# The first product of each expert from seven block products in place of eight, and the experts in two halves of d_ff

## The chip, the cores and the metric

The kernel runs on one core of a Trainium2 chip. The metric is the time of one execution on the device in microseconds (us), the median of several runs. The engines are called as in the profile: PE multiplies matrices, PEld is its loading of the stationary operand, DVE is the vector engine, ACT the scalar engine, POOL the third elementwise engine, and SP issues the DMAs.

## The reference, cut to what matters

Linear attention over 2 batches, 8 heads, 576 tokens of 64 features gives `x`, 1152 x 512. A gated layer without a nonlinearity follows, and then four experts over all tokens:

```python
x = attn_out.transpose(0, 2, 1, 3).reshape(1152, 512)
a = x @ w1; b = x @ w2                 # d_ff 1024
x = (a * b @ w3) @ w_out               # back to 512
p = domain_probs / (domain_probs.sum(-1, keepdims=True) + 1e-09)
for e in range(4):
    h = np.maximum(x @ moe2_w1[e], 0.0)        # first product:  1152 x 512 by 512 x 1024
    out += p[:, e:e + 1] * (h @ moe2_w2[e])    # second product: 1152 x 1024 by 1024 x 512
```

All inputs are float32.

## The kernel before, in words

**Numbers.** A product of float32 values is made from three matmuls. `split` turns a tile into a high part (ACT rounds it into the matmul's format, L70) and a low part (DVE subtracts that from the source, L71), and `PASSES` adds low x high, high x low and high x high in one PSUM bank. Every tile that enters a matmul has both parts, `[:, HI]` and `[:, LO]`.

**Stages.** First comes the attention, pair of heads by pair of heads, with the folding of `w3 @ w_out` beside it (`fold`, L175). Then `gated` (L148) makes `a * b` for each batch and block of d_ff, and `expert_input(b)` (L193) multiplies it by the folded weights, which gives `x2[b, j]`: for batch `b` the 128 rows `j` of d_model, transposed, 576 tokens wide. Each batch is worked in two columns of 288 tokens (`c`). From there on only the experts run.

**An expert.** For each block of 128 columns of d_ff (`g`, in two quarters `qd`), 4 banks take the first product for 2 batches x 2 columns, each from 4 blocks of d_model x 3 passes, 288 columns a matmul (L485). The two columns `c` follow each other with the same stationary tile. ACT takes relu of a bank as the high part of `hid` (L492), DVE the low part from the same bank (L493). When the 8 blocks of `hid` are there, the second product runs over 9 tiles of 128 tokens, each a chain of 24 matmuls of 512 columns (L504), and DVE adds the bank, times the expert's weight, to `acc` (L510 for the first expert, L512 for the others). After the last expert each tile of `acc` goes out by DMA (L517).

**Weights.** `load_w` brings 128 x 512 of weights by a DMA on SP into one of 4 buffers of the pool `raw` (L469) and splits it into a tile of `w1` (8 buffers, one expert's halves in turn) or `w2e` (8 buffers). The buffer of `raw` is free for the next load when the low part has been made.

**Order.** The program's text is not the order on the engines: a scheduler puts all instructions of an engine into one fixed list before the kernel runs, and each engine goes through its list without overtaking. Banks of PSUM are taken in turn: eight of them, called t, f, kv, et, f, x, w, po (f twice).

Of the kernel before, what the change touches and what calls it, by code (L numbers as in the profile page):

```python
# [8 lines left out]
F32 = mybir.dt.float32  # L9
# [26 lines left out]
def attention_moe_kernel(ctx: ExitStack, tc: tile.TileContext, q, k, v, omega, mw1, mw2, mw3, mwo, probs, ew1, ew2, out):  # L36
# [28 lines left out]
    def bank(tag):  # L65
        return ps_p.tile([P, 512], F32, tag=tag, name="ps_" + tag, bufs=BANKS[tag])
# [370 lines left out]
    a_p = mctx.enter_context(tc.tile_pool(name="a", bufs=1, reuse_waits="tile"))  # L437
# [29 lines left out]
    def load_w(pool, src, name):  # L467
        r = raw_p.tile([P, 512], F32, tag="raw", name=name + "r")
        nc.sync.dma_start(out=r, in_=src)  # L469
        t = pool.tile([P, 2, 512], F32R, tag=pool.name, name=name)  # L470
        split(t[:, HI], t[:, LO], r)
        return t

    for e in range(NE):
        hd = []
        for qd in range(EFF // 512):
            w1t = [load_w(w1_p, ew1[e, kk * P:(kk + 1) * P, qd * 512:(qd + 1) * 512], "w1") for kk in range(KD)]
            for g in range(4):
                ht = hid_p.tile([P, 2, NT], F32R, tag="hid", name="hid")
                banks = [next_bank() for _ in range(2 * B)]  # L480
                for b in range(B):
                    for kk in range(KD):
                        for n, (x, y) in enumerate(PASSES):
                            for c in range(2):
                                nc.tensor.matmul(  # L485
                                    out=banks[2 * b + c][:, :HS], lhsT=w1t[kk][:, x, g * P:(g + 1) * P],
                                    rhs=x2[b, kk][:, y, c * HS:(c + 1) * HS],
                                    start=(kk == 0 and n == 0), stop=(kk == KD - 1 and n == 2),
                                )
                for c in range(2 * B):  # L490
                    s = slice(c * HS, (c + 1) * HS)
                    nc.scalar.activation(out=ht[:, HI, s], in_=banks[c][:, :HS], func=ACTF.Relu)  # L492
# [4 lines left out]
                hd.append(ht)
        w2t = [load_w(w2_p, ew2[e, f * P:(f + 1) * P, :], "w2") for f in range(KE)]
        for t in range(NTILE):
            ps = next_bank()  # L500
            n = 0
            for f in range(KE):
                for x, y in PASSES:
                    nc.tensor.matmul(  # L504
                        out=ps, lhsT=hd[f][:, x, t * P:(t + 1) * P], rhs=w2t[f][:, y], start=(n == 0), stop=(n == 3 * KE - 1),
                    )
                    n += 1
            p_e = pr[:, t, e:e + 1]
            if e == 0:
                nc.vector.tensor_scalar(out=acc[:, t], in0=ps, scalar1=p_e, scalar2=None, op0=ALU.mult)  # L510
            else:
                nc.vector.scalar_tensor_tensor(  # L512
                    out=acc[:, t], in0=ps, scalar=p_e, in1=acc[:, t], op0=ALU.mult, op1=ALU.add,
                )
            if e == NE - 1:
                for rows, toks in out_rows(t):
                    nc.sync.dma_start(out=out[toks], in_=acc[rows, t])  # L517
# [30 lines left out]
```

## Time and profile before

| | us |
|---|---|
| median of 3 runs | 731.67 |
| lowest and highest of them | 729.31, 731.77 |
| the profiled execution | 733.19 |
| its span, first to last instruction | 731.4 |
| PE busy | 706.1 |
| DVE busy | 321.8 |
| ACT busy | 228.7 |

The profiled execution is 1.5 us above the median and 1.8 us longer than its own span. Matmuls are pipelined, and the profile shows each until its end, so that a matmul of 288 columns has a length of 295 ns while the next one starts 130 ns after it.

### The profile page before, as it was taken

How to read it: one execution, taken by the hardware profiler on the slowest of the kernel's cores; microseconds unless marked ns; L12 is line 12 of the kernel's file. 1: busy time of each engine (PE TensorE's matmuls, PEld its weight loads, DVE VectorE, ACT ScalarE, POOL GpSimd, SP SyncE). 2: the span in 40 equal slices, each digit the busy share in tenths (PEclk: the TensorE clock that was granted, in tenths of full speed). 3: DMA queues.
4: the chain of work that ended last, by engine and by line, in shares of the span. 5: the costliest groups of instructions: out<-in, count | busy, mean ns of one | idle time of the engine just before them, and what ended most of it. 6: DMA issues, size and time to landing. Idle time of an engine off the chain costs nothing.

```text
span 731.4 us, 10840 instructions
## 1 busy us (share of the span) xinstructions
PE 706.1 (97%) x4457; PEld 649.0 (89%) x4457; DVE 321.8 (44%) x620; ACT 228.7 (31%) x524; POOL 47.8 (7%) x47
## 2 busy tenths in 40 slices
PE   6879999989899999999999999999999999999997
PEld 5768888879899999999998899988899988999886
DVE  3799667689942275315331154231334311522111
ACT  4675545466422254214330033210223200322000
POOL 1130000035300041000000000000000000000000
PEclk9989999999999999999999999999999999999999
DMA  7676343345410031203110031020211200100011
GB/s 198 193 201 186 103 117 101 101 144 173 145 59 1 1 116 47 70 1 116 59 58 1 1 116 58 1 57 1 71 46 58 58 0 1 58 1 1 30 49 53
DMA packets 44129, 52.13 MB, mean 71 GB/s; under 512 B 15280, under 2 KB 31664, under 8 KB 44080
## 3 DMA queue, kind: packets, MB, share of 16 engines
q1 hardware_dynamic: 44080, 51.44, 23.4%
q8 instruction: 35, 0.57, 0.3%
q14 instruction: 14, 0.11, 0.1%
HBM read 49.07 MB, written 2.36 MB: 70 GB/s over the span
## 4 chain that ended last, share of the span: by engine, by line
PE 74%; issue 8%; DVE 8%; DMA 5%; ACT 1%; POOL 1%; DVEq 0%; POOLq 0%; SPq 0%; ACTq 0%
PE ps_f L504 7%; PE ps_f L485 7%; PE ps_po L175 5%; DMA f<-in_moe_w_dram 4%; PE ps_kv L504 4%; PE ps_et L504 4%; PE ps_po L485 3%; PE ps_x L485 3%; PE ps_et L485 3%; PE ps_t L485 3%; PE ps_w L485 3%; PE ps_kv L485 3%; PE ps_t L504 3%; PE ps_po L504 3%; PE ps_w L504 3%
## 5 line engine op out<-in xcount | busy, mean ns | idle before, releaser
L485 PE MATMUL ps_f<-x,w 128*128 128x288 f32 x384 | 102.7, 295 | 0.0
L485 PEld LDWEIGHTS ps_f<-x,w 128*128 128x128 f32 x384 | 72.3, 188 | 0.1
L70 ACT ACTIVATE w<-w2r 128x512 fp32r<-128x512 f32 x32 | 19.9, 632 | 140.1 <-PE ps_et L504 44.5
L504 PE MATMUL ps_f<-w,hid 128*128 128x512 f32 x240 | 56.1, 389 | 0.0
L504 PEld LDWEIGHTS ps_f<-w,hid 128*128 128x128 f32 x240 | 44.9, 188 | 9.2
L148 PE MATMUL ps_po<-xt,w 128*128 128x288 f32 x240 | 49.6, 305 | 2.7 <-DVE w3o L71 2.1
L485 PE MATMUL ps_w<-x,w 128*128 128x288 f32 x192 | 51.4, 295 | 0.0
L485 PE MATMUL ps_t<-x,w 128*128 128x288 f32 x192 | 51.4, 295 | 0.0
L485 PE MATMUL ps_kv<-x,w 128*128 128x288 f32 x192 | 51.4, 295 | 0.0
L485 PE MATMUL ps_po<-x,w 128*128 128x288 f32 x192 | 51.4, 295 | 0.0
L485 PE MATMUL ps_x<-x,w 128*128 128x288 f32 x192 | 51.4, 295 | 0.0
L485 PE MATMUL ps_et<-x,w 128*128 128x288 f32 x192 | 51.3, 295 | 0.0
L148 PE MATMUL ps_w<-xt,w 128*128 128x288 f32 x240 | 48.7, 297 | 0.9 <-DVE a L159 0.9
L175 PE MATMUL ps_po<-wo,w3T 128*128 128x512 f32 x192 | 48.6, 402 | 0.3 <-DVE w3T L71 0.2
L71 POOL TENSOR_TENSOR w<-w12f,w 128x512 fp32r<-128x512 f32 x24 | 35.1, 1469 | 183.7 <-ACT w L70 91.7
L175 PEld LDWEIGHTS ps_po<-wo,w3T 128*128 128x128 f32 x192 | 35.2, 188 | 8.6 <-DVE w3T L71 1.6
L148 PEld LDWEIGHTS ps_po<-xt,w 128*128 128x128 f32 x240 | 39.2, 194 | 3.4 <-DVE w3o L71 2.2
L85 DVE SCALAR_TENSOR_TENSOR f64e<-f,f64e 128x512 uint32<-128x512 uint32 x48 | 40.1, 837 | 0.6
L148 PEld LDWEIGHTS ps_w<-xt,w 128*128 128x128 f32 x240 | 38.7, 191 | 1.5 <-DVE a L159 0.7
L84 DVE TENSOR_SCALAR f64e<-f 128x512 uint32<-128x512 uint32 x48 | 24.6, 514 | 27.3 <-DMA f<-in_moe_w_dram 26.4
L485 PEld LDWEIGHTS ps_kv<-x,w 128*128 128x128 f32 x192 | 36.2, 189 | 0.0
L485 PEld LDWEIGHTS ps_w<-x,w 128*128 128x128 f32 x192 | 36.2, 189 | 0.0
(185 smaller groups left out, 1390.1 us busy)
## 6 DMA issues: line engine op xcount, KB each, us to landing
f<-in_moe_w_dram SPq DMA_DIRECT2D x40, 512.0 KB, 3.7
w1r<-in_moe_w_dram SPq DMA_DIRECT2D x32, 256.0 KB, 3.0
w2r<-in_moe_w_dram SPq DMA_DIRECT2D x32, 256.0 KB, 2.8
f<-in_moe_w_out_dram SPq DMA_DIRECT2D x8, 512.0 KB, 4.8
kr<-in_k_dram SPq DMA_DIRECT2D x8, 256.0 KB, 3.3
va<-in_v_dram SPq DMA_DIRECT2D x16, 128.0 KB, 4.0
qr<-in_q_dram SPq DMA_DIRECT2D x8, 256.0 KB, 3.7
out_dram<-acc SPq DMA_DIRECT2D x8, 256.0 KB, 2.1
```

The source lines that it names most:

```text
L70: nc.scalar.activation(out=hi, in_=src, func=ACTF.Copy)
L71: (eng or nc.vector).tensor_tensor(out=lo, in0=src, in1=hi.bitcast(F32), op=ALU.subtract)
L84: nc.vector.tensor_scalar(out=e, in0=high, scalar1=0x80000000, scalar2=None, op0=ALU.bitwise_and)
L85: nc.vector.scalar_tensor_tensor(out=e, in0=low, scalar=29, in1=e, op0=ALU.logical_shift_right, op1=ALU.bitwise_or)
L148: nc.tensor.matmul(out=bs[c][:, :HS], lhsT=w12[w, g][:, x, kk], rhs=xt[b][kk][:, y, c * HS:(c + 1) * HS], start=(kk == 0 and n == 0), stop ...
L175: nc.tensor.matmul(out=po, lhsT=wt[:, a, g * P:(g + 1) * P], rhs=wo[hf * 4 + g][:, c], start=(n == 0), stop=(n == 3 * KF - 1),)
L485: nc.tensor.matmul(out=banks[2 * b + c][:, :HS], lhsT=w1t[kk][:, x, g * P:(g + 1) * P], rhs=x2[b, kk][:, y, c * HS:(c + 1) * HS], start=(k ...
L504: nc.tensor.matmul(out=ps, lhsT=hd[f][:, x, t * P:(t + 1) * P], rhs=w2t[f][:, y], start=(n == 0), stop=(n == 3 * KE - 1),)
```

## The change: what it does

The first product of an expert is a matrix of 1024 (d_ff) x 1152 (tokens). The change cuts d_ff, d_model and the tokens in two each (the tokens by batch), so that the product is 2 x 2 blocks by 2 x 2 blocks, `A11` to `A22` of the weights (rows: half of d_ff, columns: half of d_model) and `B11` to `B22` of the tokens (rows: half of d_model, columns: batch). Written out, that is eight block products; Winograd's form has seven, with sums of the operands before and of the products behind:

- of the weights: S1 = A21 + A22, S2 = S1 - A11, S3 = A11 - A21, S4 = A12 - S2
- of the tokens: T1 = B12 - B11, T3 = B22 - B12, T2 = B22 - T1, T4 = B21 - T2
- products: P1 = A11 B11, P2 = S2 T2, P3 = S3 T3, P4 = S1 T1, P5 = A12 B21, P6 = A22 T4, P7 = S4 B22
- results: C11 = P1 + P5; u2 = P1 + P2, u3 = u2 + P3; c22 = u3 + P4, c21 = u3 + P6, c12 = u2 + P4 + P7

The sums of the tokens are made once, in `expert_input`, and those of the weights for each expert. `hidden(g, c)` makes one block of 128 rows of both halves of d_ff for one column `c` of both batches: seven products of 6 matmuls each. P5, P6 and P7 are accumulated in the banks of P1, P3 and P4, which hold their first product until ACT (for P1) or DVE (for P3 and P4) has read it. Each expert runs in two halves (`hf`): a half makes 4 of the 8 blocks of `hid` and then adds its part of the second product to `acc`, so that a chain of the second product has 12 matmuls and `acc` takes 9 additions a half.

`hid` has 4 buffers in place of 8, `w2e` 6, and the pools of the last stage lie on the other side of the memory. The core of the diff:

```diff
     def expert_input(b):
-        for j in range(KD):
-            x2[b, j] = xt_p.tile([P, 2, S], F32R, tag="xt", name="x2")
...
+                j = i // 2 + i % 2 * (KD // 2)
...
-                split(x2[b, j][:, HI, s], x2[b, j][:, LO, s], ps[:, :HS])
+                p = ps[:, :HS]
+                if b == 0:
...
+                    nc.scalar.activation(out=xf[j][:, s], in_=p, func=ACTF.Copy)
+                    put_x2(("B11", "B21")[i % 2], i // 2, s, xf[j][:, s])
+                elif i % 2 == 0:
...
+                    nc.vector.tensor_tensor(out=t1, in0=p, in1=xf[j][:, s], op=ALU.subtract)
+                    put_x2("T1", i // 2, s, t1)
+                else:
+                    b22 = temp("b22")
+                    nc.scalar.activation(out=b22, in_=p, func=ACTF.Copy)
+                    nc.vector.tensor_tensor(out=t3, in0=b22, in1=top, op=ALU.subtract)
+                    nc.vector.tensor_tensor(out=t1, in0=b22, in1=t1, op=ALU.subtract)
+                    put_x2("B22", i // 2, s, b22)
+                    put_x2("T3", i // 2, s, t3)
+                    put_x2("T2", i // 2, s, t1)
+                    nc.vector.tensor_tensor(out=t1, in0=xf[j][:, s], in1=t1, op=ALU.subtract)
+                    put_x2("T4", i // 2, s, t1)
...
+    GH = KE // 4
+    w2_p = ctx.enter_context(tc.tile_pool(name="w2e", bufs=6, side="right", reuse_waits="tile"))
+    hid_p = ctx.enter_context(tc.tile_pool(name="hid", bufs=2 * GH, side="right", reuse_waits="tile"))
...
+    def load_w1(hf):
+        raw = {}
+        for m, k in ((1, 0), (1, 1), (0, 0), (0, 1)):
+            r = raw_p.tile([P, 2, GH * P], F32, tag="raw", name="w1r")
+            f0 = m * (EFF // 2) + hf * GH * P
+            nc.sync.dma_start(
+                out=r, in_=ew1[e, k * (DM // 2):(k + 1) * (DM // 2), f0:f0 + GH * P].rearrange("(k p) f -> p k f", p=P),
+            )
+            raw[f"A{m + 1}{k + 1}"] = r
...
+            nc.vector.tensor_tensor(out=r, in0=x, in1=y, op=op)
+            w1s(name, r)
+        for name in ("A11", "A12", "A22"):
+            w1s(name, raw[name])
...
+    def hidden(g, c):
...
+        def product(ps, a, b, first=True, final=True):
+            for kk in range(2):
+                for n, (x, y) in enumerate(PASSES):
+                    nc.tensor.matmul(
+                        out=ps, lhsT=w1t[a][:, x, kk, g * P:(g + 1) * P], rhs=x2[b, kk][:, y, s],
...
+        pa, pb, pc, pd = (next_bank()[:, :HS] for _ in range(4))
+        product(pa, "A11", "B11", final=False)
+        p1 = s_p.tile([P, HS], F32, tag="p1", name="p1", bufs=2)
+        nc.scalar.activation(out=p1, in_=pa, func=ACTF.Copy)
+        product(pb, "S2", "T2")
+        u2 = total(pb, p1, "u2")
+        product(pc, "S3", "T3", final=False)
+        u3 = total(pc, u2, "u3")
+        product(pd, "S1", "T1", final=False)
+        c22 = total(pd, u3, "c22")
+        product(pa, "A12", "B21", first=False)
+        put(0, 0, pa)
+        put(1, 1, c22)
+        product(pc, "A22", "T4", first=False)
+        put(1, 0, total(pc, u2, "c21"))
+        product(pd, "S4", "B22", first=False)
+        put(0, 1, total(pd, u2, "c12"))
...
     for e in range(NE):
-        hd = []
-        for qd in range(EFF // 512):
...
+        for hf in range(2):
+            w1t, w2t = {}, []
+            load_w1(hf)
+            hd = [hid_p.tile([P, 2, NT], F32R, tag="hid", name="hid") for _ in range(2 * GH)]
+            for c in range(2):
+                for g in range(GH):
+                    hidden(g, c)
+            blocks = [m * (KE // 2) + hf * GH + g for m in range(2) for g in range(GH)]
+            w2t = [load_w2(f) for f in blocks]
...
+            for t in (0, 1, 5, 6, 2, 3, 4, 7, 8):
```

`put` is relu as the high part (ACT) and the low part (DVE) from its source, and `total` is one addition on DVE. Three places in the engines' lists show what the scheduler makes of it.

The first is PE's list at the start of the first product: of the second expert before the change, of the second half of the first expert with it. Names are bank, tokens, weights; `x3` is three matmuls in a row. In the change w1_4005 is A11, 3992 S2, 3997 S3, 3987 S1, 4008 A12. Before:

```order
L485 MATMUL ps_kv_4269<-x2_2400,w1_4250 128x288
L485 MATMUL ps_et_4270<-x2_2400,w1_4250 128x288
L485 MATMUL ps_kv_4269<-x2_2400,w1_4250 128x288
L485 MATMUL ps_et_4270<-x2_2400,w1_4250 128x288
L485 MATMUL ps_kv_4269<-x2_2400,w1_4250 128x288
L485 MATMUL ps_et_4270<-x2_2400,w1_4250 128x288
```

With the change:

```order
L556 MATMUL ps_kv_4018<-x2_2428,w1_4005 128x288 x3
L556 MATMUL ps_kv_4018<-x2_2488,w1_4005 128x288 x3
L556 MATMUL ps_et_4019<-x2_3253,w1_3992 128x288 x3
L556 MATMUL ps_et_4019<-x2_3326,w1_3992 128x288 x3
L556 MATMUL ps_f_4020<-x2_3254,w1_3997 128x288 x3
L556 MATMUL ps_f_4020<-x2_3327,w1_3997 128x288 x3
L556 MATMUL ps_x_4021<-x2_3252,w1_3987 128x288 x3
L556 MATMUL ps_x_4021<-x2_3325,w1_3987 128x288 x3
L556 MATMUL ps_w_4084<-x2_2428,w1_4005 128x288 x3
L556 MATMUL ps_w_4084<-x2_2488,w1_4005 128x288 x3
L556 MATMUL ps_kv_4018<-x2_2458,w1_4008 128x288 x3
L556 MATMUL ps_kv_4018<-x2_2518,w1_4008 128x288 x3
```

Two banks in alternation have become runs of six matmuls in one bank. Behind P1 to P4 of the first block (kv, et, f, x) stands P1 of the second block (w), and only then P5 of the first (kv again).

The second place is DVE's list where one second product ends and the next first product begins: behind the first expert before the change, behind its first half with it. `w2_` rows are low parts of w2, `acc` rows the additions to `acc`. Before:

```order
L510 TENSOR_SCALAR acc_3445<-ps_t_4196,pr_80 128x512
L71 TENSOR_TENSOR w2_4778<-w2r_4776,w2_4778 128x512
L71 TENSOR_TENSOR w2_4783<-w2r_4781,w2_4783 128x512
L71 TENSOR_TENSOR w2_4788<-w2r_4786,w2_4788 128x512
L71 TENSOR_TENSOR w2_4793<-w2r_4791,w2_4793 128x512
L71 TENSOR_TENSOR w2_4798<-w2r_4796,w2_4798 128x512
L510 TENSOR_SCALAR acc_3445<-ps_f_4222,pr_80 128x512
L71 TENSOR_TENSOR w2_4803<-w2r_4801,w2_4803 128x512
L71 TENSOR_TENSOR w2_4808<-w2r_4806,w2_4808 128x512
L71 TENSOR_TENSOR w2_4813<-w2r_4811,w2_4813 128x512
L493 SCALAR_TENSOR_TENSOR hid_4268<-ps_kv_4269,hid_4268 128x288
```

With the change (the sums S2, S3 and S4 are those of the half after the one that begins here):

```order
L80 TENSOR_TENSOR w2_4294<-w2r_4292,w2_4294 128x512
L80 TENSOR_TENSOR w2_4299<-w2r_4297,w2_4299 128x512
L615 TENSOR_SCALAR acc_3525<-ps_f_3963,pr_80 128x512
L539 TENSOR_TENSOR S2_4441<-S1_4436,w1r_4432 128x512
L539 TENSOR_TENSOR S3_4446<-w1r_4432,w1r_4428 128x512
L571 TENSOR_TENSOR u2_4036<-ps_et_4019,p1_4028 128x288
L539 TENSOR_TENSOR S4_4451<-w1r_4434,S2_4441 128x512
L571 TENSOR_TENSOR u3_4044<-ps_f_4020,u2_4036 128x288
L571 TENSOR_TENSOR c22_4052<-ps_x_4021,u3_4044 128x288
L565 SCALAR_TENSOR_TENSOR hid_4014<-ps_kv_4018,hid_4014 128x288
L571 TENSOR_TENSOR u2_4102<-ps_po_4085,p1_4094 128x288
L80 TENSOR_TENSOR w2_4735<-w2r_4733,w2_4735 128x512
```

The sums of the next weights stand ahead of and between u2, u3 and c22, for which PE's P6 and P7 wait.

The third place is SP's list at the same point, with the queues that each load waits for; a load that needs a buffer of `raw` waits for the queue of the load that had it before, and for DVE's last reading. The low part of w2r_4292 waits for the same DMAHW7. Before:

```order
L469 DMA w2r_4801<-in_moe2_w2_dram 128x512 [waits DMAHW2_49,DVE_49]
L469 DMA w2r_4806<-in_moe2_w2_dram 128x512 [waits DMAHW3_49,DVE_49]
L469 DMA w2r_4811<-in_moe2_w2_dram 128x512 [waits DMAHW4_49,DVE_49]
L469 DMA w1r_5050<-in_moe2_w1_dram 128x512 [waits DMAHW5_49,DVE_49]
L469 DMA w1r_5055<-in_moe2_w1_dram 128x512 [waits DMAHW6_49,DVE_49]
```

With the change:

```order
L517 DMA w2r_4292<-in_moe2_w2_dram 128x512 [waits DMAHW6_49,DVE_49]
L517 DMA w2r_4297<-in_moe2_w2_dram 128x512 [waits DMAHW3_49,DVE_49]
L528 DMA w1r_4428<-in_moe2_w1_dram 128x2x256 [waits DMAHW4_49,DVE_49]
L528 DMA w1r_4430<-in_moe2_w1_dram 128x2x256 [waits DMAHW2_49,DVE_49]
L528 DMA w1r_4432<-in_moe2_w1_dram 128x2x256 [waits DMAHW7_49,DVE_49]
L528 DMA w1r_4434<-in_moe2_w1_dram 128x2x256 [waits DMAHW0_49,DVE_49]
L517 DMA w2r_4733<-in_moe2_w2_dram 128x512 [waits DMAHW1_49,DVE_49]
L517 DMA w2r_4738<-in_moe2_w2_dram 128x512 [waits DMAHW5_49,DVE_49]
```

Loads of w1 now stand four and four with those of w2, as 256 columns of two blocks of d_model, and w1r_4432 (A11) takes the buffer of w2r_4292.

## Rows read from the trace of the kernel before

**Rows 1.** The page, part 1: busy us, share of the span, instructions.

```profile
PE 706.1 (97%) x4457; PEld 649.0 (89%) x4457; DVE 321.8 (44%) x620; ACT 228.7 (31%) x524; POOL 47.8 (7%) x47
```

**Rows 2.** Windows, second expert: length, PE, PEld, DVE, ACT, POOL busy, clock, DMA.

```profile
426.90:478.00 51.10, 51.10 (x385) 51.10 (x384) 19.52 (x41) 16.94 (x41) 0.00 (x0) 1.00 0.17 51
478.00:527.30 49.30, 49.30 (x221) 40.85 (x220) 10.76 (x16) 4.45 (x9) 0.00 (x0) 1.00 0.12 33
```

**Rows 3.** Windows with L485 alone: length, PE busy, PEld busy, clock, DMA.

```profile
327.90:378.00 50.10, 50.05 (x384) 49.90 (x384) 1.00 0.21 64
426.80:478.20 51.40, 51.34 (x384) 51.13 (x384) 1.00 0.17 51
527.00:579.00 52.00, 51.35 (x384) 51.11 (x383) 1.00 0.18 57
627.00:679.00 52.00, 51.34 (x384) 51.27 (x384) 1.00 0.03 10
```

**Rows 4.** The same with L504 alone, second product of the first expert.

```profile
377.80:427.40 49.60, 49.15 (x216) 40.43 (x216) 1.00 0.13 36
```

**Rows 5.** The same with L193 alone, expert_input of the second batch.

```profile
300.00:328.50 28.50, 25.60 (x192) 25.50 (x192) 1.00 0.07 20
```

**Rows 6.** Timeline of PE where L485 goes to new banks: start, length.

```profile
330.94 0.29 PE L485 MATMUL ps_kv<-x,w 128*128 128x288 f32 x1
...
331.07 0.29 PE L485 MATMUL ps_et<-x,w 128*128 128x288 f32 x1
```

**Rows 7.** Groups by line: busy us, mean ns, idle before and its releasers.

```profile
L71 DVE TENSOR_TENSOR w<-w2r,w 128x512 fp32r<-128x512 f32 x32 | 21.6, 690 | 9.8 <-ACT w L70 9.7
...
L70 ACT ACTIVATE w<-w2r 128x512 fp32r<-128x512 f32 x32 | 19.9, 632 | 140.1 <-PE ps_et L504 44.5 <-PE ps_f L504 43.1 <-PE ps_kv L504 43.1
...
L493 DVE SCALAR_TENSOR_TENSOR hid<-ps_f,hid 128x288 fp32r<-128x288 f32 x32 | 14.5, 452 | 27.2 <-ACT hid L492 27.2
...
L492 ACT ACTIVATE hid<-ps_f 128x288 fp32r<-128x288 f32 x32 | 13.1, 408 | 29.9 <-PE ps_f L485 29.9
...
L159 DVE TENSOR_TENSOR a<-ps_w,a 128x288 f32<-128x288 f32 x14 | 6.4, 454 | 19.6 <-PE ps_w L148 19.5
...
L512 DVE SCALAR_TENSOR_TENSOR acc<-ps_f,pr,acc 128x512 f32<-128x512 f32 x7 | 5.3, 750 | 32.5 <-PE ps_f L504 32.5
```

**Rows 8.** Timeline of DVE in the gated stage: start, length, idle before.

```profile
283.38 0.46 DVE L159 TENSOR_TENSOR a<-ps_w,a 128x288 f32<-128x288 f32 x1 [1.23 <-PE ps_w L148]
283.75 0.45 DVE L159 TENSOR_TENSOR a<-ps_po,a 128x288 f32<-128x288 f32 x1
284.18 0.69 DVE L71 TENSOR_TENSOR w<-w1r,w 128x512 fp32r<-128x512 f32 x1
284.79 0.82 DVE L71 TENSOR_TENSOR hid<-a,hid 128x288 fp32r<-128x288 f32 x2
```

**Rows 9.** Timeline where loads wait for the four buffers of raw.

```profile
422.96 2.73 DVE L71 TENSOR_TENSOR w<-w2r,w 128x512 fp32r<-128x512 f32 x4 [0.59 <-ACT w L70]
423.68 2.37 SPq L469 DMA_DIRECT2D w2r<-in_moe_w_dram  x4
426.48 1.26 ACT L70 ACTIVATE w<-w2r 128x512 fp32r<-128x512 f32 x2 [1.51 <-DMA w2r<-in_moe_w_dram]
```

**Rows 10.** DMA issues: count, KB each, median us from issue to landing.

```profile
w1r<-in_moe_w_dram SPq DMA_DIRECT2D x32, 256.0 KB, 3.0
w2r<-in_moe_w_dram SPq DMA_DIRECT2D x32, 256.0 KB, 2.8
f<-in_moe_w_out_dram SPq DMA_DIRECT2D x8, 512.0 KB, 4.8
kr<-in_k_dram SPq DMA_DIRECT2D x8, 256.0 KB, 3.3
```

**Rows 11.** Windows of the attention stage, columns as in rows 2.

```profile
36.00:55.00 19.00, 14.82 (x86) 11.92 (x85) 17.60 (x34) 14.02 (x33) 6.34 (x5) 0.88 0.69 194
...
200.00:327.00 127.00, 126.44 (x951) 125.91 (x951) 52.44 (x102) 39.79 (x94) 13.01 (x10) 1.00 0.14 43
```

**Rows 12.** Timeline of the end.

```profile
727.56 0.75 DVE L512 SCALAR_TENSOR_TENSOR acc<-ps_f,pr,acc 128x512 f32<-128x512 f32 x1 [4.69 <-PE ps_f L504]
```

More of the change, by code (lines that the diff above doesn't have):

```diff
@@ L184, in expert_input @@
     def expert_input(b):
-        for j in range(KD):
-            x2[b, j] = xt_p.tile([P, 2, S], F32R, tag="xt", name="x2")
         for c in range(2):
             s = slice(c * HS, (c + 1) * HS)
-            for j in range(KD):
-                ps = bank(ALL_BANKS[c][j])
+            for i in range(KD):
+                j = i // 2 + i % 2 * (KD // 2)
+                ps = bank(ALL_BANKS[c][i])
                 for kk in range(KF):
@@ L435, in attention_moe_kernel @@
                         gated(at, 2, int(s[1]), int(s[2]), ("w", "po") * 2)
[L437 removed]
+    xq_p = ctx.enter_context(tc.tile_pool(name="xq", bufs=1, reuse_waits="tile"))
+    a_p = mctx.enter_context(tc.tile_pool(name="a", bufs=1, reuse_waits="tile", side="right"))
     for t in range(NTILE):
@@ L465, in next_bank, with load_w2 @@
         return bank(("t", "f", "kv", "et", "f", "x", "w", "po")[turn[0] % 8])
[L467 to L470, printed above, removed]
+    def load_w2(f):
+        r = raw_p.tile([P, 512], F32, tag="raw", name="w2r")
+        nc.sync.dma_start(out=r, in_=ew2[e, f * P:(f + 1) * P, :])
+        t = w2_p.tile([P, 2, 512], F32R, tag="w2e", name="w2")
@@ L471, in load_w @@
         split(t[:, HI], t[:, LO], r)
         return t
-    for e in range(NE):
-        hd = []
-        for qd in range(EFF // 512):
[L477 to L492, printed above, removed]
+    def load_w1(hf):
[7 more added lines that the diff above has]
+            raw[f"A{m + 1}{k + 1}"] = r
+        sums = {}
+        for name, x, y, op in (
+            ("S1", "A21", "A22", ALU.add), ("S2", "S1", "A11", ALU.subtract), ("S3", "A11", "A21", ALU.subtract),
+            ("S4", "A12", "S2", ALU.subtract),
+        ):
+            r = sums[name] = s_p.tile([P, 2, GH * P], F32, tag="s", name=name, bufs=3)
+            x, y = (raw.get(i) or sums[i] for i in (x, y))
+            nc.vector.tensor_tensor(out=r, in0=x, in1=y, op=op)
+            w1s(name, r)
+        for name in ("A11", "A12", "A22"):
+            w1s(name, raw[name])
@@ new lines, in attention_moe_kernel @@
+    for e in range(NE):
+        for hf in range(2):
[7 more added lines that the diff above has]
+            w2t = [load_w2(f) for f in blocks]
+            last = e == NE - 1 and hf == 1
+            for t in (0, 1, 5, 6, 2, 3, 4, 7, 8):
+                ps = next_bank()
+                n = 0
+                for i in range(len(blocks)):
+                    for x, y in PASSES:
+                        nc.tensor.matmul(
+                            out=ps, lhsT=hd[i][:, x, t * P:(t + 1) * P], rhs=w2t[i][:, y], start=(n == 0), stop=(n == 3 * len(blocks) - 1),
+                        )
+                        n += 1
+                p_e = pr[:, t, e:e + 1]
+                if e == 0 and hf == 0:
+                    nc.vector.tensor_scalar(out=acc[:, t], in0=ps, scalar1=p_e, scalar2=None, op0=ALU.mult)
+                else:
@@ L493, in attention_moe_kernel @@
                     nc.vector.scalar_tensor_tensor(
-                        out=ht[:, LO, s], in0=banks[c][:, :HS], scalar=0.0, in1=ht[:, HI, s].bitcast(F32),
-                        op0=ALU.max, op1=ALU.subtract,
-                    )
[L497 to L517, printed above, removed]
@@ L521 @@
+                        out=acc[:, t], in0=ps, scalar=p_e, in1=acc[:, t], op0=ALU.mult, op1=ALU.add,
+                    )
+                if last:
+                    for rows, toks in out_rows(t):
+                        nc.sync.dma_start(out=out[toks], in_=acc[rows, t])
 _INS = ['q', 'k', 'v', 'omega', 'moe_w1', 'moe_w2', 'moe_w3', 'moe_w_out', 'moe2_domain_probs', 'moe2_w1', 'moe2_w2']
```

46 lines of the change are left out of this document (39 added, 7 removed).

## The prediction

> **What bounds the kernel now.** I began with the page: PE is busy 706.1 us of 731.4, DVE 44% and ACT 31% [rows 1]. That busy PE may still be waiting inside its pipeline, so I went on to the windows of the experts, where the change is. In the second expert PE has no gap in either product, while DVE works 19.5 us of 51.1 and 10.8 us of 49.3 [rows 2]. The first product alone takes 50.05, 51.34, 51.35 and 51.34 us for 384 matmuls each [rows 3], the second 49.15 us for 216 [rows 4]. So from about 328 us to the end the time is a number of matmuls times a price: 204.08 / 1536 = 0.133 us for one of 288 columns, 49.15 / 216 = 0.2275 us for one of 512. Going to another bank costs nothing when it is free: the first matmul into a new bank starts 0.13 us after the last one into the old [rows 6]. What removes a matmul here removes its price, as long as the other engines keep up.
>
> **What the change removes.** The first product goes from 4 x 384 = 1536 matmuls to 4 experts x 2 halves x 4 blocks x 7 products x 6 = 1344, and PE's list holds that many; the second stays at 864. What is one of the 1344 worth? They come in runs of six in one bank with another stationary tile each time, where before two banks alternated over the same tile. The nearest row for that form is expert_input, whose runs of 24 in one bank change the tile each time: 25.60 / 192 = 0.1333 us [rows 5]. Bounds are the first expert's 50.05 / 384 = 0.1303 and the third's 51.35 / 384 = 0.1337 [rows 3]. At 0.1333 the product takes 179.2 us, and 204.1 - 179.2 = **24.9 us** go. At the bounds it is 28.9 and 24.4 us. I take the middle one, since its form is the same.
>
> **What it adds, and what hides it.**
>
> *DVE, in total.* A half has 4 blocks of 9 operations of 288 columns (five sums, four low parts), 4 sums of weights and 11 low parts of weights of 512, and 9 additions to acc. Before, 288 columns take 0.45 us with a source in PSUM [rows 7], and two from SBUF take 0.82 us together [rows 8]; 512 take 0.69 us, an addition to acc 0.75 us [rows 7]. So 36 x 0.45 + 15 x 0.69 + 9 x 0.75 = 33.3 us for a half, in which PE needs 168 x 0.1333 + 108 x 0.2275 = 47.0 us. ACT has 20 x 0.41 + 11 x 0.63 = 15.1 us. Neither is the bound by its sum, and nothing stands in the way of PE but the order of DVE's list. The nine additions to acc are twice as many as before and lie under chains of 12 x 0.2275 = 2.7 us each.
>
> *DVE, inside a block.* P6 and P7 go into banks that DVE must first have read. In PE's list P1 to P4 of the first block are followed by P1 of the second, P5 of the first, and P2 to P4 of the second, so that P6 comes 53 matmuls (7.1 us) after the half's start, though P3 was done after 18 (2.4 us). The scheduler has put the other block's work into the gap.
>
> *DVE, at the start of a half.* Here the list is tight, because three loads follow each other through DVE. I count from the half's first matmul. The last token's chain lets go of the oldest tile of w2 nine matmuls earlier, at -2.05 + 0.16 = -1.9. ACT's high part takes it to -1.25, DVE's low part to -0.55, and that frees the buffer of raw for A11. A freed buffer's load is issued within 0.1 us and used 2.8 us later [rows 9]; the median for w1 is 3.0 us [rows 10]. So A11 is there at 2.45, S2 and S3 end at 3.85, u2 at 4.3, S4 at 5.0, u3 at 5.45, c22 at 5.9. PE asks for u3 at 7.1 and for c22 at 7.9. S3 frees A21's buffer for a tile of w2: landed at 6.65, high part 7.3, low part 8.0, behind it u3 of the second block at 8.9; asked for after 78 matmuls, at 10.4. That low part frees the buffer for the next tile of w2: 10.8, 11.4, 12.1, and behind it stand eight operations of 0.45 us up to u3 of the third block, 15.7; asked for after 126 matmuls, at 16.8. The least slack is 1.1 us, or 0.8 us less the nine hand-overs of about 0.03 us [rows 9]. Operations that wait for nothing start 0.37 us apart in place of 0.45 [rows 8], which gives some back. There are six such starts (the last half has no next weights, the first comes out of another stage). By these rows they cost nothing; since 0.8 us is little over three loads, I charge **1.0 us** in all. Bounds: nothing, and what the second rival gives.
>
> *The first half.* DVE still has the last sums of the tokens, four low parts of w2 and the sums of the next weights. The latest point is c12 of the first block: after the last product of expert_input come a copy (0.41) and its wake (0.2), two sums, four low parts of 512 and then 17 operations of 288 and 6 of 512, together 0.6 + 0.9 + 2.8 + 7.7 + 4.1 = 16.1 us. PE asks for that bank after 120 matmuls, at 16.0 us. I charge **0.5 us**; the bounds are nothing and 2 us.
>
> *The rest at nothing.* The end of the half needs its low parts for the fourth token at the earliest, since 0, 1 and 5 lie in the first column; that is 8.2 us of cover, and without it DVE's last two or three microseconds would be seen once a half. The sums of the tokens in expert_input (36 operations, 16.2 us, with 7.6 us of weights) lie under 25.6 us of PE [rows 5]. Copies of the first batch by ACT lie beside the gated stage, where ACT works 39.8 of 127 us [rows 11]. The end is as before, one addition after the last chain [rows 12], and a DMA. The four early loads of w1 have the same bytes in shorter rows.
>
> **The sum.** -24.9 + 0.5 + 1.0 = -23.4 us. The profiled execution of 733.19 us becomes 709.8 us, with a span of 708.0; it was 1.5 us above the median of the runs, and the median of 731.67 us becomes **708.3 us**.
>
> **The rivals.**
>
> *First: DVE's list runs late at each half.* For it speaks the small slack; against it that loads in the experts' stage land in 2.8 to 3.0 us with the DMA at 0.17 of its time [rows 2, 10]. Loads of w1 now have rows of half the length; the nearest of that kind, of k, land in 3.3 us [rows 10]. Three at 3.3 us add 0.3 + 0.5 + 0.5 = 1.3 us, less 0.8 of slack, six times: 3.0 us, a median near 710. At 4.0 us each it is 3.4 - 0.8 = 2.6 us, six times 15.6, and a median of 723. So this case reaches from 711 to 728.
>
> *Second, on the other side: three landings of 4.8 us.* That is what loads of w_out take in the attention stage [rows 10]. They add 1.8 + 2.0 + 2.0 = 5.8 us, less 0.8, six times: 30 us, which is 731.67 - 24.4 + 30 = 737. The gain is used up from 4.9 us of added landing at a half's start, about 4.5 us a load. Those are 512 KB a load in a stage with the DMA at 0.69 of its time [rows 11], against 256 KB and 0.17 here [rows 2], so I give it little.
>
> *Third: PE's clock.* It was granted in full from 200 us on, where PE has next to no gap, but 0.88 on average from 36 to 55 us, where PE was idle 4.2 of 19 us in pieces between its matmuls [rows 11]; of the two levels, 2.4 and 1.2 GHz, the lower was there a part of that time. If the waits inside the seven products did the same to the first product, its 179.2 us would take 179.2 / 0.88 - 179.2 = 24.4 us more, and the median would be 732.7: no change. Against it: by the count above those waits are met before PE comes to them. The Trainium skill, "TensorE: Matmul & The Clock Gate", section "A second HAM failure mode: psum-queue depth-cycling", speaks against this change: a kernel that goes round its banks with small gaps between groups of matmuls was seen to lose and regain the clock again and again. By that rule the third rival would be the forecast; the trace from 328 us on goes round eight banks at full clock, but with no gaps, so it does not settle what small gaps would do.
>
> *That the change does not do what it says* is out: PE's list has 1344 and 864 matmuls.
>
> **How the numbers follow.** The forecast, 703 to 711 us, has 0.72: from the price of 0.1303 (731.7 - 28.9 = 702.8) up to the upper bound of the first half and loads of 3.3 us. The first rival has 0.17, spread from 711 to 728; the second 0.05; the third, or something else that leaves no change, 0.04; a gain beyond 29 us 0.02. The range 703 to 718 takes the forecast and nearly half of the first rival, about 0.8. A measurement of this kernel can tell 0.5%, 3.7 us, from no change. Faster: 0.72 + 0.17 + 0.02 = 0.91; same 0.04; slower 0.05.
>
> **What would show it.** Right, if the first product has 1344 matmuls at about 0.133 us and the windows of a half show PE without gaps for some 47 us, with DVE busy around 33 us of them. The tight place shows as idle time of PE ahead of the accumulating products, released by DVE's u3 or c22, some 7, 10 and 17 us into a half; the releaser behind DVE would be the landing of w1r or w2r. A granted clock under 1.00 after 330 us would speak for the third rival. The forecast is wrong if matmuls with a new stationary tile in short runs cost more than 0.134 us, or if DVE's operations with one source in PSUM and one in SBUF take longer than 0.45 us.

## The result and the profile after

The changed kernel takes 706.58 us (median of 705.21 to 711.43), the kernel before 731.72 beside it: a ratio of 0.9664, 95% interval 0.9602 to 0.9726. The forecast was 708.3 us.

The page of the changed kernel, part 1, answers to [rows 1]:

```profile
PE 685.3 (97%) x4265; PEld 627.0 (88%) x4265; DVE 453.7 (64%) x900; ACT 267.0 (38%) x604; POOL 47.9 (7%) x47
```

PE has 192 matmuls less; DVE has 280 operations and 132 us of work more, and still is not what is waited for. The experts now begin at 331.00 us and their last matmul ends at 705.75. Windows over halves of experts, with the columns of [rows 2]; the first, second, third and last of eight:

```profile
331.00:378.00 47.00, 47.00 (x280) 42.68 (x279) 35.03 (x72) 18.19 (x41) 0.00 (x0) 1.00 0.19 57
378.00:424.83 46.83, 46.83 (x279) 42.56 (x278) 30.43 (x61) 14.20 (x31) 0.00 (x0) 1.00 0.16 46
424.83:471.65 46.82, 46.82 (x278) 42.55 (x278) 30.45 (x61) 14.19 (x31) 0.00 (x0) 1.00 0.15 46
...
658.93:705.75 46.82, 46.81 (x276) 42.19 (x275) 21.91 (x46) 8.18 (x20) 0.00 (x0) 1.00 0.13 46
```

In every half PE is busy for the whole length, at full clock; DVE is busy 30.4 us of a middle half, 35.0 of the first window and 21.9 of the last. No half shows idle time, and PE's list of waits has no row of the experts. Eight halves are 374.75 us; before, the experts took from 327.95 to 727.5, 399.5 us. So the stage gave 24.8 us.

The third half again, with the first product's line alone and then with the second's alone; they answer to [rows 3, 4]:

```profile
424.83:471.65 46.82, 22.60 (x170) 22.49 (x170) 1.00 0.15 46
...
424.83:471.65 46.82, 24.88 (x108) 20.16 (x108) 1.00 0.15 46
```

22.60 / 170 = 0.1329 us for a matmul of the first product (two of the 170 belong to the half behind). The second line can't be divided so: with the two products interleaved, the modelled end of one run lies over the start of the next. What the 168 leave of the half, 46.82 - 22.3 = 24.5, is 0.2268 us for each of the 108.

The start of that half, on the timeline (start, length, engine, what it waited for):

```profile
423.48 1.37 DVE L80 TENSOR_TENSOR w<-w2r,w 128x512 fp32r<-128x512 f32 x2 [0.59 <-ACT w L79]
424.20 1.05 SPq L528 DMA_DIRECT2D w1r<-in_moe_w_dram  x2
424.66 0.95 PE L556 MATMUL ps_et<-x,w 128*128 128x288 f32 x6
...
426.93 0.69 DVE L539 TENSOR_TENSOR S<-S,w1r 128x512 f32<-128x512 f32 x1 [1.32 <-DMA w1r<-in_moe_w_dram]
...
428.51 0.68 DVE L539 TENSOR_TENSOR S<-w1r,S 128x512 f32<-128x512 f32 x1
...
429.11 0.45 DVE L571 TENSOR_TENSOR u<-ps_x,u 128x288 f32<-128x288 f32 x1
...
431.64 0.95 PE L556 MATMUL ps_x<-x,w 128*128 128x288 f32 x6
...
438.93 0.45 DVE L571 TENSOR_TENSOR u<-ps_x,u 128x288 f32<-128x288 f32 x1
...
441.32 0.96 PE L556 MATMUL ps_x<-x,w 128*128 128x288 f32 x6
```

This is the tight place of the prediction. A low part frees the buffer, the load of A11 is issued at 424.20, DVE waits 1.32 us for it and makes S2 at 426.93, S3 and, at 428.51, S4, and u3 of the first block is done at 429.11 + 0.45 = 429.56. PE comes to that bank at 431.64: 2.1 us to spare. For the third block it is 439.38 against 441.32, 1.9 us. The wait is real, and it lies on DVE alone.

Loads in the experts, count, KB, median us to landing, beside [rows 10]:

```profile
w1r<-in_moe_w_dram SPq DMA_DIRECT2D x28, 256.0 KB, 2.7
w2r<-in_moe_w_dram SPq DMA_DIRECT2D x28, 256.0 KB, 2.6
```

The rows of half the length that the loads of w1 now have did not make them later.

The profiled execution took 711.43 us and began its experts 3.05 us later than the one before did. PE's list is the same in both programs for its first 1175 matmuls, up to the gated stage; the next one starts at 210.0 us before and at 213.1 us here, so the difference arises ahead of it, in the attention stage. Its windows from 45 to 65 us:

```profile
45.00:55.00 10.00, 7.01 (x32) 5.33 (x31) 9.63 (x22) 6.63 (x15) 4.46 (x3) 0.83 0.66 182
55.00:65.00 10.00, 10.00 (x41) 9.18 (x40) 6.21 (x12) 4.78 (x12) 1.26 (x1) 0.50 0.54 161
```

and the second of them in the kernel before, then in the changed kernel when it was run once more:

```profile
55.00:65.00 10.00, 9.82 (x65) 9.04 (x64) 9.93 (x18) 7.65 (x20) 1.43 (x1) 0.88 0.73 200
...
55.00:65.00 10.00, 8.42 (x61) 7.71 (x60) 9.07 (x16) 8.19 (x20) 1.48 (x2) 1.00 0.83 232
```

For all of those ten microseconds the chip granted 0.50 in the first execution, the lower of the two levels (1.2 GHz), and PE got through 41 matmuls where the same program later did 61 at 1.00. That later execution began its experts at 327.4 us. So these microseconds come and go between executions; they are no part of the change.

### The profile page after: what moved, and what is told of

It is laid out like the page before. It is cut to its first block, busy times and chain, and to the rows that moved or that the text cites. A ratio compares the mean times of both kernels' runs of the same rounds, so it can differ in the third digit from the quotient of the medians.

```text
span 709.6 us, 10874 instructions
## 1 busy us (share of the span) xinstructions
PE 685.3 (97%) x4265; PEld 627.0 (88%) x4265; DVE 453.7 (64%) x900; ACT 267.0 (38%) x604; POOL 47.9 (7%) x47
## 4 chain that ended last, share of the span: by engine, by line
PE 87%; DVE 5%; DMA 3%; ACT 1%; issue 1%; POOL 0%; SPq 0%; ACTq 0%; POOLq 0%; DVEq 0%
PE ps_f L609 7%; PE ps_f L556 6%; PE ps_po L184 6%; PE ps_po L157 4%; PE ps_x L609 3%; PE ps_t L609 3%; PE ps_et L609 3%; PE ps_po L609 3%; PE ps_w L609 3%; PE ps_kv L609 3%; PE ps_f L267 3%; PE ps_x L556 3%; PE ps_w L556 3%; PE ps_kv L556 3%; PE ps_et L556 3%; PE ps_t L556 3%
## 5 line engine op out<-in xcount | busy, mean ns | idle before, releaser
L564 ACT ACTIVATE hid<-c 128x288 fp32r<-128x288 f32 x96 | 41.9, 438 | 48.1 <-DVE c L571 47.8
L556 PE MATMUL ps_f<-x,w 128*128 128x288 f32 x336 | 52.8, 295 | 0.0
L556 PEld LDWEIGHTS ps_f<-x,w 128*128 128x128 f32 x336 | 47.5, 188 | 0.2
L565 DVE SCALAR_TENSOR_TENSOR hid<-c,hid 128x288 fp32r<-128x288 f32 x96 | 43.3, 453 | 4.8 <-ACT hid L564 1.5
L273 DVE TENSOR_REDUCE mx<-ps_f 128x4 f32<-128x512 f32 x34 | 22.9, 678 | 14.2 <-PE ps_f L267 10.8
L80 DVE TENSOR_TENSOR w<-w2r,w 128x512 fp32r<-128x512 f32 x32 | 21.8, 691 | 14.3 <-ACT w L79 14.3
L79 ACT ACTIVATE w<-S 128x512 fp32r<-128x512 f32 x32 | 19.4, 627 | 22.6 <-DVE S L539 18.8
L556 PE MATMUL ps_x<-x,w 128*128 128x288 f32 x168 | 27.3, 295 | 0.0
L556 PE MATMUL ps_t<-x,w 128*128 128x288 f32 x168 | 27.3, 295 | 0.0
L556 PE MATMUL ps_w<-x,w 128*128 128x288 f32 x168 | 27.3, 295 | 0.0
```

The source lines that it names most:

```text
L79: nc.scalar.activation(out=hi, in_=src, func=ACTF.Copy)
L80: (eng or nc.vector).tensor_tensor(out=lo, in0=src, in1=hi.bitcast(F32), op=ALU.subtract)
L273: top = nc.vector.tensor_reduce(out=mx, in_=pv, op=ALU.max, axis=AX.X, negate=True)
L556: nc.tensor.matmul(out=ps, lhsT=w1t[a][:, x, kk, g * P:(g + 1) * P], rhs=x2[b, kk][:, y, s], start=(first and kk == 0 and n == 0), stop=(f ...
L564: nc.scalar.activation(out=h[:, HI, o], in_=src, func=ACTF.Relu)
L565: nc.vector.scalar_tensor_tensor(out=h[:, LO, o], in0=src, scalar=0.0, in1=h[:, HI, o].bitcast(F32), op0=ALU.max, op1=ALU.subtract,)
```

## The experiments

**Theory.** PE bounds the experts without a gap, so the gain is 192 matmuls at 0.13 us; what the change adds on DVE and in the loads lies in slack. **Rivals.** The gain comes from working in halves, with their smaller tiles; or DVE's list, tight as it is at each half's start, is nearly the bound. Since the part ahead of the experts moves by some microseconds from one execution to the next, I read each run by the experts' length in its trace as well, from the first matmul of the first product to the end of the last one:

| run | median us | ratio to before, interval | experts begin | take | against 374.75 |
|---|---|---|---|---|---|
| halves, eight products | 733.00 | 1.0018, 0.9999 to 1.0037 | 327.0 | 400.2 | +25.5 |
| seven, one issued twice | 733.81 | 1.0011, 0.9984 to 1.0037 | 328.2 | 400.1 | +25.4 |
| three more sums a block | 711.53 | 0.9742, 0.9690 to 0.9795 | 326.5 | 378.0 | +3.3 |
| six more sums a block | 720.51 | 0.9846, 0.9830 to 0.9862 | 327.9 | 386.9 | +12.2 |
| three raw buffers | 710.96 | 0.9709, 0.9675 to 0.9743 | 330.0 | 374.8 | 0.0 |
| banks four and four | 716.97 | 0.9774, 0.9725 to 0.9824 | 333.2 | 378.6 | +3.9 |
| loads of w1 twice | 714.56 | 0.9759, 0.9710 to 0.9807 | 332.5 | 375.1 | +0.4 |
| loads in shorter rows | 708.07 | 0.9653, 0.9622 to 0.9684 | 328.3 | 374.8 | 0.0 |
| the change again | 707.97 | 0.9665, 0.9602 to 0.9727 | 327.4 | 374.8 | 0.0 |

**The halves alone.** The kernel before, with the experts' loops as the change has them:

```diff
-    w2_p = ctx.enter_context(tc.tile_pool(name="w2e", bufs=KE, reuse_waits="tile"))
-    hid_p = ctx.enter_context(tc.tile_pool(name="hid", bufs=KE, reuse_waits="tile"))
+    w2_p = ctx.enter_context(tc.tile_pool(name="w2e", bufs=6, reuse_waits="tile"))
+    hid_p = ctx.enter_context(tc.tile_pool(name="hid", bufs=KE // 2, reuse_waits="tile"))
...
-            for t in range(NTILE):
+            for t in (0, 1, 5, 6, 2, 3, 4, 7, 8):
...
-                for f in range(KE):
+                for f in range(4):
```

> The kernel before with its experts in two halves of d_ff, as the change has them (four hidden buffers, six of the second weights, the second product of 12 matmuls after each half, the same order of the token tiles), but with all eight block products, so 1536 matmuls of the first product. Theory (the gain is the 192 matmuls that are no longer issued, at about 0.13 us each): the time of the kernel before, about 731 us, within 3 us. Rival (the halves, with their smaller transfers and buffers, give the gain): about 707 us, and PE's experts stage near 375 us in place of 399.6. Where the halves cost something of their own, it shows here as an experts stage above 399.6 us.

Its experts, a first stretch and the sum over four:

```profile
327.00:427.00 100.00, 100.00 (x606) 91.54 (x605) 42.10 (x75) 26.98 (x59) 0.00 (x0) 1.00 0.19 59
...
sum 400.24, PE 400.24 PEld 366.07 DVE 145.51 ACT 83.17 POOL 0.00; mean PE 100.06 PEld 91.52 DVE 36.38 ACT 20.79 POOL 0.00
```

PE has no gap and needs 400.2 us, 0.7 more than before (399.5). The halves give nothing; that rival is out.

**The eighth product back.** The changed kernel, with one line more:

```diff
         product(pb, "S2", "T2")
+        product(pb, "S2", "T2")
```

> The changed kernel with one of its seven products (S2 with T2) issued twice in each of the 32 blocks, so that TensorE issues 1536 matmuls of the first product again and computes the same. Theory: 192 matmuls at 0.133 us come back, +25.5 us to 732 us, and PE still has no gap in the experts. Rival (TensorE is not what bounds the experts; VectorE's list or the loads are): the added matmuls are partly hidden in waits, and the time rises by less than 15 us, to below 722 us.

```profile
628.00:728.28 100.28, 100.28 (x602) 91.34 (x600) 52.20 (x104) 21.89 (x50) 0.00 (x0) 1.00 0.12 38
sum 400.28, PE 400.28 PEld 365.77 DVE 242.21 ACT 112.14 POOL 0.00; mean PE 100.07 PEld 91.44 DVE 60.55 ACT 28.04 POOL 0.00
```

Everything else of the change is still there, DVE works 242 us in place of the 146 above, and the whole gain is gone: 192 matmuls cost 25.4 us, 0.132 each. From either side the gain is these matmuls, to within a microsecond.

**More work on DVE.** Two kernels issue the sum u3 four and seven times:

```diff
-            nc.vector.tensor_tensor(out=t, in0=x, in1=y, op=ALU.add)
+            for _ in range(4 if name == "u3" else 1):
+                nc.vector.tensor_tensor(out=t, in0=x, in1=y, op=ALU.add)
```

> The changed kernel with the sum u3 issued four times in place of once in each of the 32 blocks (same result): VectorE gets 12 more sums of 288 columns in a half, 4.4 to 5.4 us at 0.37 us apart or 0.45 us long, on the 30.4 us that it is busy of 46.8. Theory 1 (VectorE has some 16 us to spare in a half, and about 1.9 us at the start of one, which three sums of 0.37 us use up in each block): by the third block of a half u3 is 3.3 us later, 1.4 us more than its slack, so PE waits up to 1.4 us at each of seven later halves: 707 to 717 us. Theory 2 (only the sum over a half counts, the scheduler's distance between blocks hides the rest): no change, 706 to 708 us. Rival (VectorE is already nearly the bound): all of it appears, +35 to +43 us, about 745 us.

> The changed kernel with u3 issued seven times in place of once in each block (same result): 24 more sums in a half, 8.9 to 10.8 us on VectorE, which then is busy 39 to 41 us of a half's 46.8. Theory 1 (what binds is the order of VectorE's list at the start of a half, with a slack of 1.9 us): by the third block u3 is 6.7 us later, 4.8 us more than its slack, at each of seven or eight halves: +34 to +38 us, 741 to 745 us. Theory 2 (only the sum over a half counts): still hidden, 706 to 710 us. Rival (VectorE is already the bound): +71 to +86 us.

Windows of the kernel with three more sums:

```profile
326.50:374.00 47.50, 45.66 (x270) 41.00 (x269) 37.40 (x81) 17.25 (x39) 0.00 (x0) 1.00 0.18 56
374.00:421.00 47.00, 47.00 (x276) 42.54 (x275) 34.86 (x73) 14.28 (x31) 0.00 (x0) 1.00 0.16 46
```

Its timeline of PE in the first half, at two points of the second, and DVE's last u3 and PE's return to that bank in the first block of the third:

```profile
336.53 1.06 PE L556 MATMUL ps_f<-x,w 128*128 128x288 f32 x6 [0.33 <-DVE hid L565]
338.15 1.06 PE L556 MATMUL ps_f<-x,w 128*128 128x288 f32 x6 [0.56 <-ACT p L578]
340.16 1.06 PE L556 MATMUL ps_et<-x,w 128*128 128x288 f32 x6 [0.95 <-DVE u L572]
...
376.75 0.43 PE L556 MATMUL ps_kv<-x,w 128*128 128x288 f32 x2
...
394.50 1.09 PE L610 MATMUL ps_et<-w,hid 128*128 128x512 f32 x4
...
429.36 0.45 DVE L572 TENSOR_TENSOR u<-ps_x,u 128x288 f32<-128x288 f32 x1
...
431.96 0.95 PE L556 MATMUL ps_x<-x,w 128*128 128x288 f32 x6
```

Three waits in the first half, none in the seven behind it, although DVE there works 34.9 us of 47. From 335.24 to 342.02 five groups that take 0.79 us each without a wait took 6.78 us: 2.8 of the 3.3 us. The total, 711.53 us, lies in the range of my first theory (707 to 717 us), but by luck: that theory had put 1.4 us at each of seven later halves, and only the first half paid, which has no second product of an earlier half ahead of it. The program is not the same with a longer DVE list. In the third half the last of the four u3 ends at 429.81 and PE comes to that bank at 431.96, 8.8 us after the half's first matmul (423.12), where the changed kernel comes 7.0 us after it (424.66 to 431.64); so PE still finds u3 done, 2.1 us ahead. The second product begins earlier too, 17.8 us after the half's first matmul (376.75 to 394.50) where the changed kernel has 20.7 (471.48 to 492.14). That this other order is why the later halves paid nothing is how I read it; no run holds the order fixed under more work.

With six more sums the first half and the second pay. PE in the first half:

```profile
338.94 1.06 PE L556 MATMUL ps_f<-x,w 128*128 128x288 f32 x6 [0.56 <-ACT p L578]
342.27 1.81 PE L556 MATMUL ps_f<-x,w 128*128 128x288 f32 x6 [2.27 <-DVE hid L565]
344.09 1.81 PE L556 MATMUL ps_et<-x,w 128*128 128x288 f32 x6
```

Windows around the longest wait, the granted clock third from the end:

```profile
327.90:338.90 11.00, 10.48 (x80) 10.24 (x78) 10.35 (x24) 6.50 (x15) 0.00 (x0) 1.00 0.38 117
338.90:342.27 3.37, 1.06 (x6) 0.83 (x7) 3.37 (x9) 0.93 (x2) 0.00 (x0) 0.94 0.04 13
342.27:348.58 6.31, 6.30 (x24) 5.95 (x25) 5.76 (x15) 2.13 (x6) 0.00 (x0) 0.50 0.23 83
348.58:356.00 7.42, 7.42 (x48) 6.89 (x48) 6.95 (x17) 3.21 (x7) 0.00 (x0) 0.99 0.00 1
```

The wait of 2.27 us costs more than itself: behind it the granted clock is 0.50, 1.2 GHz, until 348.58, and 24 matmuls take 6.31 us in place of 3.2. From 337.40 to 349.42 the loss is 12.02 - 7 x 0.79 = 6.5 us; two waits in the second half, around 393 and 396.6, make 2.7 more, at full clock:

```profile
376.00:424.00 48.00, 45.85 (x272) 41.31 (x271) 36.57 (x81) 14.23 (x32) 0.00 (x0) 1.00 0.15 45
```

The other 3 us are spread over the stage, and I have not told them apart. Neither theory gave 720 us: DVE with some 39 us of 48 is no longer hidden everywhere, and yet 9 of the 12 us come from two halves of eight.

**One buffer fewer for loads.**

```diff
-    raw_p = ctx.enter_context(tc.tile_pool(name="raw", bufs=4))
+    raw_p = ctx.enter_context(tc.tile_pool(name="raw", bufs=3))
```

> The changed kernel with three buffers for loaded weights in place of four (same result). The first sum of a half, S1, then cannot be made before the end of the half ahead: its two loads stand behind the last low part of the second product's weights, so four serial loads in place of three lie at a half's start. Theory of the prediction's step (d) (VectorE's sums of loaded weights must be made in the first 4 to 6 us of a half; about 1.9 us of slack): one more landing of 2.7 us and one sum of 0.7 us, 3.4 us less 1.9 us of slack: up to 1.5 us at each of seven halves, +0 to +11 us, 707 to 718 us, and waits of PE for VectorE's u sums in the waits list. Rival (the order that the scheduler writes gives way, by putting more of the second product's matmuls ahead): no wait of PE, 706 to 708 us.

The start of a half in its timeline:

```profile
423.65 0.95 PE L556 MATMUL ps_et<-x,w 128*128 128x288 f32 x6
...
426.01 0.69 DVE L539 TENSOR_TENSOR S<-w1r 128x512 f32<-128x512 f32 x1 [1.41 <-DMA w1r<-in_moe_w_dram]
...
428.19 0.45 DVE L571 TENSOR_TENSOR u<-ps_x,u 128x288 f32<-128x288 f32 x1
...
430.63 0.95 PE L556 MATMUL ps_x<-x,w 128*128 128x288 f32 x6
431.05 0.69 DVE L539 TENSOR_TENSOR S<-w1r,S 128x512 f32<-128x512 f32 x1 [0.35 <-DMA w1r<-in_moe_w_dram]
```

S1 now stands at the half's start and waits for its loads, as expected, but S4, which stood ahead of u3 in the changed kernel, stands behind the sums of the blocks, at 431.05. So u3 is done at 428.64, again 2.0 us ahead of PE. The experts take 374.8 us: the rival's case, the order gives way.

**Blocks in four banks.**

```diff
-        return bank(("t", "f", "kv", "et", "f", "x", "w", "po")[turn[0] % 8])
+        return bank(("t", "f", "kv", "f")[turn[0] % 4])
...
-        pa, pb, pc, pd = (next_bank()[:, :HS] for _ in range(4))
+        pa, pb, pc, pd = (bank(x)[:, :HS] for x in ("x", "et", "w", "po"))
```

> The changed kernel with four of the eight banks for the first product's blocks alone and four for the second product (same result), so that no two blocks stand in flight in free banks. Theory (the waits inside a block are covered because the scheduler lays matmuls of another block, or of the second product, between P3 and P6): with the second product as the only other work the half's last blocks are covered and its first are not; a block alone has P6 30 matmuls, 4.0 us, behind the start of P1, and needs two sums (0.9 us) and one copy (0.6 us) behind 18 matmuls: it still fits, so 0 to 1 us a block, 706 to 725 us. Rival (the list of VectorE has no room, every block waits): over 1 us for each of 32 blocks, above 738 us.

```profile
336.52 1.06 PE L556 MATMUL ps_x<-x,w 128*128 128x288 f32 x6
337.81 1.06 PE L556 MATMUL ps_et<-x,w 128*128 128x288 f32 x6 [0.23 <-DVE u L571]
338.92 1.06 PE L556 MATMUL ps_w<-x,w 128*128 128x288 f32 x6
340.24 1.05 PE L556 MATMUL ps_x<-x,w 128*128 128x288 f32 x6 [0.27 <-DVE hid L565]
```

From 335.52 to 341.14 five groups take 5.62 us, 1.7 more than 5 x 0.79; from there on PE has no gap. Most of the other 2 us of the 3.9 is no wait: from start to start a matmul of the second product takes 0.2295 us on average where the changed kernel has 0.2273, in every half; why, I have not tested. The rest of what this kernel took more lies ahead of the experts, which begin at 333.2 us in its trace although PE's list up to there is that of the changed kernel. So in the experts two blocks in flight are worth little: where the second product lies between, one block at a time does nearly as well.

**Later landings.** One kernel issues each load of w1 twice, one behind the other, into the same buffer; another takes the same bytes in rows of 128 columns and so reads other weights, with every engine's list as in the changed kernel.

```diff
-            nc.sync.dma_start(
+            for _ in range(2):
+                nc.sync.dma_start(
...
```

```diff
-                out=r, in_=ew1[e, k * (DM // 2):(k + 1) * (DM // 2), f0:f0 + GH * P].rearrange("(k p) f -> p k f", p=P),
+                out=r.rearrange("p k (b f) -> p (k b) f", f=128), in_=ew1.rearrange("e d f -> (e d) f")[0:512, f0:f0 + 128].rearrange("(k p) f -> p k f", p=P),
```

> The changed kernel with each of the 32 loads of the first product's expert weights issued twice into the same buffer, the second behind the first (same result): a landing of 2.8 us becomes one of some 5.6 us, and SP's queue is held meanwhile. The prediction's second rival gave +3.6 us a half (737 us in all) from landings of 4.8 us. If that mechanism holds, seven later halves with landings of 5.6 us give +25 us and more: above 730 us, with waits of PE for VectorE's sums at the start of each half. Theory (the scheduler's order gives way, and the loads are issued earlier): below 715 us, with waits in the first half at most.

> The changed kernel with the loads of the first product's expert weights taken from rows of 128 columns in place of 256, as many bytes in twice as many packets; it reads other weights than it should, so its output is another, while every engine's instructions stand in the same order as in the changed kernel. So the landing gets longer by an amount to be read from the trace, with the order held fixed. Theory (u3 of a half's first blocks has 1.9 to 2.1 us of slack behind the load of A11): a landing longer by less than 1.9 us costs nothing, the experts stage stays at 374.8 us; each us above that costs 7 us over the seven later halves. Rival (the prediction's second: landings of 4.8 us cost 3.6 us a half): a landing of 4 us already costs over 1 us a half, an experts stage above 382 us.

The start of a half with the loads doubled:

```profile
426.06 3.79 SPq L529 DMA_DIRECT2D w1r<-in_moe_w_dram  x4
426.52 0.95 PE L557 MATMUL ps_et<-x,w 128*128 128x288 f32 x6
...
429.09 0.46 DVE L572 TENSOR_TENSOR u<-ps_x,u 128x288 f32<-128x288 f32 x1 [0.26 <-PE ps_x L557]
429.88 0.46 DVE L572 TENSOR_TENSOR c<-ps_w,u 128x288 f32<-128x288 f32 x1 [0.33 <-PE ps_w L557]
...
431.54 0.69 DVE L540 TENSOR_TENSOR S<-S,w1r 128x512 f32<-128x512 f32 x1 [1.20 <-DMA w1r<-in_moe_w_dram]
```

A11 is there 5.5 us after its issue, twice as late as in the changed kernel, and nothing happens to PE (375.1 us): S2 now stands behind u3 and c22 of the first block in DVE's list. By the prediction's second rival this would have been over 730 us. (It charged 5.0 us at each of six starts; the 3.6 us a half of the two expectations is the rise from 708.3 to 737 us over eight halves.) The second kernel was to hold the order and lengthen the landing. It held the order, but its loads land like the others:

```profile
w1r<-in_moe_w_dram SPq DMA_DIRECT2D x28, 256.0 KB, 3.0
w2r<-in_moe_w_dram SPq DMA_DIRECT2D x28, 256.0 KB, 2.6
```

So it says nothing on what a landing of 5 us would cost in the changed kernel's own order. That stays open.

**The change once more.**

> The changed kernel once more, without an edit, beside the run above. Theory: the experts stage is again 374.75 us to 0.1 us, while the time varies with where the experts begin, 326 to 333 us, so 703 to 712 us. Rival (the stage itself varies by as much as the whole): an experts stage off by over 1 us.

Its experts take 374.8 us from 327.4. The stage repeats to within 0.1 us in four traces (this one, the first, three buffers, shorter rows), while the profiled executions as a whole differ by the clock in the attention stage and, where that was rescheduled too (three buffers, doubled loads), perhaps by its order. What the medians of 711 and 715 us of those two have above the changed kernel lies there as well: in their traces the experts begin at 330.0 and 332.5 us.

## Why the prediction was right

- **192 matmuls, -24.9 us.** Shown from both sides: -24.8 in the changed kernel, +25.5 and +25.4 where they are still there or come back. The price was taken as 0.1333 and is 0.1329; with all eight products the halves themselves cost 0.7 us (400.2 against 399.5), which fits that the changed kernel shows 24.8 and not 25.5.
- **DVE, 33.3 us of a half's 47.0.** It is 30.4 of 46.8 in a later half. The excess of the estimate, 2.9 us, is what 36 operations make that start 0.37 us apart when they wait for nothing [rows 8] and that I charged at 0.45. ACT has 14.2 for 15.1. That DVE isn't the bound by its sum was right, and it held with 34.9 us too.
- **Inside a block.** No wait of PE, as worked out. The reason I gave, another block's work in the gap, is one way to fill it; with banks for one block alone 1.7 us appeared in all, in the first half.
- **The start of a half, 1.0 us charged.** None was needed. I had 1.6, 1.5 and 1.1 us of slack for the three blocks; the trace has 2.1, 2.0 and 1.9. Landings of 2.7 us for 2.8 to 3.0, and operations 0.37 us apart, point that way.
- **The first half, 0.5 us charged.** None was needed: from its first matmul at 331.0 to that of the second half at 377.84 it took 46.86 us against 46.82 of the others. (The window of 47.00 us above holds 280 matmuls, four more than a half has.) It is the place that pays first when DVE gets more to do.
- **The sum.** -23.4 us forecast for the experts, -24.8 measured: the two charges, and little else. The profiled execution came 1.6 us above the forecast of 709.8 because its experts began 3.05 us later. That the median, 706.58, came 1.7 us below 708.3 fits the charges but does not show them: the same kernel gave a median of 707.97 when it was run again.
- **First and second rival.** The mechanism is there (DVE waits 1.32 us for a load with u3 queued behind it), and its price was worked out with DVE's order held fixed. That is the weak step of these rivals: with fewer buffers or later loads in the program, the order that is built moves one or more sums of weights behind the sums of the blocks. What a landing late only on the chip, unknown to the scheduler, would cost is untested.
- **Third rival.** The clock was 1.00 in all eight halves. The Trainium skill, "TensorE: Matmul & The Clock Gate", section "A second HAM failure mode: psum-queue depth-cycling", tells of a kernel that lost and regained the clock by small gaps between its groups of matmuls. The changed kernel does not try that rule, since PE goes round the banks without gaps; the kernel with three more sums does a little, and with gaps of 0.33 to 0.95 us between groups it kept 1.00 (326.50 to 374.00 above). Behind one gap of 2.27 us in the kernel with six more sums the clock was 0.50, while gaps of 1.20 and 0.95 us in its second half left it at 1.00 (376.00 to 424.00 above). So a fall behind a gap is to be had here, and the change has no such gap.

## What to carry to other kernels

Where windows show PE without a gap at full clock, the matmuls taken out gave their price here to within 3% (24.8 us of 25.5), and what was moved to other engines cost nothing as long as its waits were met before PE came: count that slack at the stage's start, where loads and in-order lists meet, not from the busy share. A slack counted in one built order is not a constant of the kernel, since a scheduler that knows of the delay builds another order; a test that adds work there tests the new order. And compare stages, not only totals, when an earlier stage varies by more than the effect that is looked for.

## What the hardware showed beside it

- After a wait of 2.27 us PE ran at half clock for another 6.3 us and lost 3.2 us more than the wait; this was seen once. In the same stage, waits of up to 1.20 us left the clock at 1.00.
- In the attention stage the same program was granted 0.50 in one execution and 1.00 in another over ten microseconds, and its experts began 3.6 us apart.
- Halving the rows of a 256 KB load from 256 to 128 columns left its landing at 3.0 us, beside 2.7.
- A matmul of 512 columns costs 0.2268 us and one of 288 costs 0.1329: 0.094 us for 224 columns, which leaves some 12 ns of each that does not depend on its length, an estimate from these two figures. The 192 matmuls gave that back as well.
